# A retention layer and a two-layer feed-forward on one core: an order table per engine, one more block of layer 1 in seven products, queries loaded in token pairs, and paced loads at the head

## The chip, the core and the metric

One core of a Trainium2 chip runs the whole program. The metric is device time in microseconds (us), the median of repeated executions; lower is better. Before the change three runs took 283.76, 284.01 and 282.91 us, so the median is 283.76 us.

The engines are named as in the profile: PE multiplies matrices (PEld loads its weights), DVE and POOL work on vectors, ACT evaluates functions, SP issues most of the transfers. SBUF is the on-chip memory with 128 partitions, PSUM the eight banks (here `bk`) that PE writes.

## The reference

```python
def _attn_ref(q, k, v):                     # 8 batches, 8 heads, 576 tokens, 64 wide
    scores = scale * np.matmul(q, k.transpose(0, 1, 3, 2))
    gamma = 1.0 - 2.0 ** (-5.0 - np.arange(H))
    Dmat = np.where(rel >= 0, gamma[:, None, None] ** rel[None, :, :], 0.0)
    return np.matmul(scores * Dmat[None], v)

def _moe_ref(x, w_in, w_out):               # x: 4608 x 512, w_in: 512 x 2048, w_out: 2048 x 512
    h = x @ w_in
    g = h * np.cos(h)
    return g @ w_out
```

The result of the first function, with the heads put side by side, is the `x` of the second. There is no softmax: the decay factors into a weight of the query's position and one of the key's position, so earlier tokens can be summed up in a 64x64 state for each head.

## The kernel before

**Tiling.** The 4608 tokens are cut into nine blocks of 512. Each block is two units `(b, g)` of 256 tokens, g = 0 or 1, of two batches; the ninth block gathers the last 64 tokens of all eight batches. For each unit the kernel loads q, k and v into staging buffers (`stgq`, `stgk`, `stgv`, `load`), scales them to bf16 with the weights of their positions (`natk`, `natv`, `qnat`, in `unit`), turns k and q round (`kt`, `qt`: on PE with `tpe` in the first two blocks, by transposing transfers in `txb` after that), multiplies keys with queries (`scores`), masks the result on DVE with a triangle of ones (`pt <- bk, tr`, L714), sums keys times values into states (`states`, copied by ACT to `sba`, `sbb`, `sbr` in `snap`), and adds masked scores times values and queries times states (`outputs`). ACT and DVE copy that to `xt`, the block's input of layer 1.

A unit is "coarse" where a chunk is 128 tokens, held as 64 partitions times a pair of neighbouring tokens (`y` is the place in the pair), and "fine" where a chunk is 64 tokens. Coarse units are those of batches 0 and 1 and the units (2,0) and (3,0); ten units are fine. In a fine unit `y` is the half of 128 tokens, and q, k and v each come in two transfers of 256 KB, whose runs in DRAM are 64 numbers (256 bytes); a coarse unit's load is one transfer of 512 KB with runs of 128 numbers.

**Layer 1 and layer 2.** `mlp1(j, f, ...)` makes one of the 16 slices of 128 hidden columns of a block with four products of 512 columns (L879), then ACT's sine shifted by a quarter turn gives the cosine (L888) and DVE multiplies (L891) into `gt`. Blocks in `SEVEN` (4 to 8) do layer 1 by Strassen and Winograd's scheme instead: `xsums` makes three sums `xs` of the block's input and overwrites a part of `xt` (DVE), `wsums1` makes the sums `tx` of `w_in` once and overwrites a part of `win` (half of them on POOL, half on DVE), and `seven1(j, g, ...)` for each of four column groups does seven products of four matmuls of 256 columns (L1008), with ACT copying partial sums (`sq`, and `bk <- bk`, L939), DVE adding (`sq <- bk, sq`, L991) and DVE or POOL multiplying into `gt` (L997). Layer 2 does all nine blocks that way (`wsums`, `wino2`, L1148), and the results go out through `os`.

**What sets the order.** The program is a list of tasks. `Graph.run` walks through a model of the five engines with durations and due times written into the code, picks among the ready tasks of each engine the one with the best priority (`prios`, moved by the table `SHIFT`), and thereby fixes, on the host and before anything runs, the order of every engine's instructions; `FETCHES`, `AHEAD`, `BOND` and `DUE` tune its choices. The chip then executes each engine's list in order, with semaphore waits where data demand them. Where the model sees PE idle for over 0.4 us early on, `emit` puts products of a constant matrix there (`warm`, L500).

**The head.** Six loads (q, k, v of the units (0,0) and (1,0)) are at the front of SP's list and wait for nothing. The four slabs of `w_in` (`load_w`, issued from POOL, cast on the way) wait for certain loads (`SLABS`); the loads of the unit (0,1) wait for slab 2 (`NEXT`), the slabs of `w_out` for the keys of (1,1), the loads of (2,0) for the third slab of `w_out`. On SP, DMA loads are issued one after the other as soon as their staging buffer is free.

Of the kernel before, what the change touches and what calls it, by code (L numbers as in the profile page):

```python
# [6 lines left out]
ALU = mybir.AluOpType  # L7
# [123 lines left out]
class Graph:  # L131


    BACKLOG = 2500
    AHEAD, FETCH = 2000, 6500
    DUE = ("ses/0.1",)
# [49 lines left out]
    @staticmethod  # L186
    def fetch(at):
        return next(f for end, f in Graph.FETCHES if at < end)

    FETCHES = ((30000, 11500), (55000, 9500), (68000, 10200), (104000, 7800), (118000, 13000), (205000, 8800), (1e9, 6500))  # L190
    MARK = 213
    ENTER, LEAVE, BOND = 95, 105, 2000
# [5 lines left out]
    @staticmethod  # L198
    def fill(gap, seen):
        return int(0.6 * (gap - 150) / 220 if seen else (gap - 300) / 430)  # L200

    def first(self, t):
        need = {}
        for b in t.allocs:
            need[b.pool] = need.get(b.pool, 0) + 1
        return all(b in self.fifo[b.pool][:need[b.pool]] for b in t.allocs if b.pool in self.fifo)
# [19 lines left out]
    def shift(self, table):  # L226

        i = 0
        for n in range(0, len(table), 3):
            i += ord(table[n]) - 35  # L230
            x = (ord(table[n + 1]) - 35) * 90 + ord(table[n + 2]) - 35
            self.tasks[i].prio += 10 * (x - 4050)

    def reset(self):
        for t in self.tasks:
            t.start, t.wait = None, len(t.deps)
            t.parts[0][4].pop("push", None)
            for b in t.bufs:
                b.slot, b.left, b.free = None, len(b.tasks), 0.0
        self.pools = {p: [0.0] * len(f) for p, f in self.pools.items()}  # L240
        self.holder = {p: [None] * len(f) for p, f in self.pools.items()}
        self.fifo = {p: list(q) for p, q in self.queues.items()}

    def run(self):
        self.reset()
        free = {e: 0.0 for e in ("pe", "act", "dve", "pool", "sp")}
        ready = {e: [] for e in free}
        seen, asked, whole = 20, {}, [False] * 8
        dma_free, port_free = 0.0, {"dve": 0.0, "pool": 0.0}
        est, order, last, mode, held = {}, [], None, "", None  # L250
        for t in self.tasks:
            est[t] = 0.0
            if not t.wait:
                ready[t.eng].append(t)

        def slots(t):

            need, when = {}, 0.0
            for b in t.allocs:
                need[b.pool] = need.get(b.pool, 0) + 1  # L260
                if b.pool in self.fifo and b not in self.fifo[b.pool][:need[b.pool]]:
                    return None
# [7 lines left out]
        def pick(e):  # L270
            cand = []
            for t in ready[e]:
                if e == "pe" and held and t is not held and (t.then or t.name[:3] != "ses"):
                    continue
                a = slots(t)
                if a is None:
                    continue
                s = max(free[e], est[t], a)
                if e == "pe" and t.count:
                    k = (seen + t.count - 443) // 256  # L280
                    if k >= 0 and 443 + 256 * k > seen and k in asked:
                        s = max(s, asked[k] + self.fetch(asked[k]) - t.dur * (443 + 256 * k - seen) / t.count)
                if t.port:
                    s = max(s, port_free["pool" if e == "dve" else "dve"])
                if t.dma is not None and e != "pool":
                    s = max(s, dma_free - self.BACKLOG)
                cand.append((s, t))
            if e == "pe" and not held:
                due = [t for t in ready[e] if all(any(f is not None and f <= free[e] + 1500 for f in self.pools[b.pool])
                                                  for b in t.allocs if b.pool != "bk") and self.first(t) and sum(b.pool == "bk" for b in t.allocs) > 2 - (t.name in self.DUE) and est[t] <= free[e] + 1500]  # L290
                due = [t for t in due if t.prio <= min(x.prio for x in ready[e]) + self.AHEAD]
                if due:
                    d = min(due, key=lambda t: t.prio)
                    cand = [(s, t) for s, t in cand if t is d or not any(b.pool == "bk" for b in t.allocs)]
                    mine = [s for s, t in cand if t is d]
                    if mine:
                        cand = [(s, t) for s, t in cand if t is d or s + t.dur <= mine[0] + 150]
            if not cand:
                return None
            t0 = min(s for s, t in cand)  # L300
            slack = 60 if e == "pe" else 40
            return min(((s, t) for s, t in cand if s <= t0 + slack), key=lambda c: (c[1].prio - self.BOND * (e == "pe" and self.switch(mode, c[1].name) == 0 and mode[:3] == "ses"), c[0]))

        n = 0
        while n < len(self.tasks):
            best = None
            for e in free:
                c = pick(e)
                if c and (best is None or c[0] < best[0]):
                    best = c  # L310
            if best is None:
                rest = [(t.name, t.eng, [b.pool for b in t.allocs]) for e in ready for t in ready[e]]
                keep = {p: [b and [(t.name, t.eng) for t in b.tasks if t.start is None] for b in h] for p, h in self.holder.items()}
                raise RuntimeError(f"the scheduler is stuck: {self.pools} {free} {[x for x in rest if x[0][:3] == 'ses']} {rest[:12]} {keep}")
            s, t = best
            e = t.eng
            if e == "pe":
                s = max(s, free[e] + self.switch(mode, t.name))
            gap = s - free["pe"]
            ready[e].remove(t)  # L320
            t.start, t.order = s, n
            n += 1
# [7 lines left out]
            if e == "pe":  # L330
# [5 lines left out]
                if k >= 0 and k not in asked:  # L336
                    asked[k] = s + t.dur * max(0, 128 + 256 * k - seen) / max(1, t.count)
                seen += t.count
            mark = 0
            for b in t.allocs:  # L340
# [8 lines left out]
                self.holder[b.pool][i] = b  # L349
# [7 lines left out]
            for b in t.bufs:  # L357
                b.left -= 1
                b.free = max(b.free, done + (230 if e == "pe" else 170))
                if not b.left:  # L360
                    self.pools[b.pool][b.slot] = b.free
                    self.holder[b.pool][b.slot] = None
            order.append(t)
            for o in t.succ:
# [3 lines left out]
                if not o.wait:  # L368
                    ready[o.eng].append(o)
# [5 lines left out]
class Kernel:  # L375
# [8 lines left out]
    SEVEN = (4, 5, 6, 7, 8)  # L384
# [3 lines left out]
    SHIFT = (  # L388
        "$|KLw3?#U,,G3(j'Xw'Q/$X((Oe$6_6w'8cY/cu/am-@X&h2/fT&^Z)u,'bK'Z/$Zt$X5)W0%Wo$Si)LO&Q8)V?&GC&>H&Xd&J="
        "&_;%hW$BL&Jk&Q#(Y3$CR&Ec&R3&I_&jf&Gz)Fi,Ul)X(&H\\%L3&V6'U{(R|$T'&K6&[,%Ev-0w%mf%hO'oe$fT$CQ%pN(^l+EV"  # L390
        "$8I*--'%V$=d$:1%=@$=-$Xp&.:$21&Yx$tv%kW$nq+wV*Sm)B_/?^&Ej)9[&,4&>V&LX&Wy)X+$Jj%ED$JH$WK&YT$1A)*k,#k"
        "$_*&3I+S^)PL$-y&9s$c%&-w(JS$<|&]L'LL'M.;=A&D<&;3&#`);o,Y`&U`._`,Yp'-@%VS$`j%$$$Y+<B=$N7'dd'c%$KF&;b"
        "$fO'U`,I99^#'Ym)ND'E*$FW%Jk%F\\.2@,sT$aT)W>(^T%T_'[Q.80&N0,/B-^B$A{%\\J&:0%CC-Vp+Ao,0z%i-%#U$+D%X-'Vi"
        "%XA$Bd%SJ&^d$Z#$JA)Sk'?#$@B)@;/66$F]&3H%-)%5r&+/%.q'DM&Zp0TU2M.&A\\&q-*Tc(D5'4P%Pu$5^%UZ*%M(9P$9a';>"
        "*g{-\\Z'Wt&\\K?kt&VZ'MP%p9(%B8GP(I''8c%.#$\\f(Z*;Y15J6(>n$Aa*B|*\\Y:Yg$R;%Vb$7e&_R,&i0dx6\\S'AW*E\\%Xx%RH"
        "(XU(4Z&:S7Wo.So&Se,^[&Xc-`K$L\\%Wp$XH$T++Zd'U<*|K.Y7,Mb'Ar&#b%S_%To%\\p$J\\%=#'7E$fZ$)'(/G%.<(7U)Qx$k6"
        "&2]&.U':a$2Y%8O%$b'=S'BS-_0$XW)L8$Z=+-j$,w6|C$|K9xJ"
# [10 lines left out]
    def __init__(self, nc, es, q, k, v, w_in, w_out, out):  # L408
# [13 lines left out]
        self.TR = {2: sb("tr2", [128, 256], BF16), 1: sb("tr1", [128, 64], BF16)}  # L422
# [8 lines left out]
        self.whole = [False] * self.POOLS["bk"]  # L431
# [4 lines left out]
    def build(self):  # L436
        self.graph()
        self.G.prios()
        self.G.shift(self.SHIFT)
# [18 lines left out]
    def emit(self, order):  # L458
# [4 lines left out]
        whole = self.whole  # L463
        for t in order:
# [8 lines left out]
            for end, fn, r, w, kw in t.parts:  # L473
                kw = dict(kw)
                after = [i.ops[0] if isinstance(i, Task) else ops[i] for i in kw.pop("after", ())]
                if "push" in kw:
                    after.append(kw.pop("push").ops[0])
                sem = kw.pop("sem", None)
# [12 lines left out]
                ops.append(self.P.add(t.eng, fn, r=[phys(k) for k in r], w=[phys(k) for k in w], sem=sem, after=after))  # L491

# [13 lines left out]
    def constants(self):  # L506
# [29 lines left out]
        for ny in (2, 1):  # L536
            n = 64 * ny * ny
            for dst, up, name in ((self.TR[ny], 0, "tr"), (self.TB[ny], 1, "tb")):
                for y in range(ny):
                    dims = ([64, 2], [1, 64]) if ny == 2 else ([1, 64],)  # L540
                    P.add("pool", lambda e, dst=dst, up=up, ny=ny, y=y, n=n, dims=dims: e.affine_select(
# [780 lines left out]
```

## Time and profile before

| | before |
|---|---|
| median of three runs | 283.76 us (282.91 to 284.01) |
| span of the profiled execution | 282.1 us |
| PE busy | 274.2 us (97%), 4088 matmuls |
| DVE, ACT, POOL busy | 226.7 (80%), 174.9 (62%), 152.8 us (54%) |
| DMA packets | 133130, 49.90 MB |

The page gives the span of the profiled execution, from its first instruction to its last, and no device time of its own for it. The span is 1.66 us under the median of the timed runs, and that distance is carried along wherever a span is turned into a time. A matmul's busy time runs from its start to the end of its way through the array, so neighbouring ones overlap in the busy column; what one costs is the distance from start to start. Idle rows name the engine or transfer that ended the wait.

### The profile page before, as it was taken

Reading aid. Unit: us, or ns where it says so; the run is one execution under the profiler, and the core shown is the slowest. Engines: PE = TensorE matmul, PEld = TensorE weight load, DVE = VectorE, ACT = ScalarE, POOL = GpSimd, SP = SyncE. Lnnn points to the kernel's source line nnn. Section 1 sums busy time; section 2 is a strip of 40 time slices with the busy share of each in tenths; the row PEclk is TensorE's granted clock in tenths of the full one; section 3 lists DMA queues with packets and bytes.
Section 4 is the critical chain, followed back from the end, with each engine's and each line's share of the span. In section 5 each row is a group of like instructions: output and inputs, shape, how many; then the busy total and the mean of one; then the engine's idle time right before and its main releaser. Section 6 shows DMA issues by size and latency. Waiting matters only on the chain.

```text
span 282.1 us, 9696 instructions
## 1 busy us (share of the span) xinstructions
PE 274.2 (97%) x4088; PEld 216.5 (77%) x4088; DVE 226.7 (80%) x389; ACT 174.9 (62%) x355; POOL 152.8 (54%) x170
## 2 busy tenths in 40 slices
PE   7899999999999999999999999999999999999995
PEld 2567576888784476458888888888888889888884
DVE  4677979989937898898969786889689979579753
ACT  4357683672446744764578767785778577777620
POOL 5452870487334745258587949783779333433410
PEclk9999999999999999999999999999999999999999
DMA  7999999999999999999999999997857002200124
GB/s 194 265 224 279 244 179 228 283 199 193 192 260 224 207 188 258 188 200 188 293 159 260 184 244 207 231 208 169 169 145 151 3 2 77 77 0 2 74 77 149
DMA packets 133130, 49.90 MB, mean 177 GB/s; under 512 B 105440, under 2 KB 128992, under 8 KB 133088
## 3 DMA queue, kind: packets, MB, share of 16 engines
q1 hardware_dynamic: 128576, 44.84, 74.1%
q0 software_dynamic: 4224, 4.19, 9.3%
q8 instruction: 32, 0.52, 0.8%
q10 hardware_dynamic: 288, 0.26, 0.3%
q14 instruction: 10, 0.08, 0.1%
HBM read 36.70 MB, written 9.44 MB: 164 GB/s over the span
## 4 chain that ended last, share of the span: by engine, by line
PE 83%; DMA 8%; DVE 5%; POOL 1%; issue 1%; ACT 0%; SPq 0%; DVEq 0%
PE bk L1148 37%; PE bk L1008 22%; PE bk L879 14%; PE bk L675 8%; DMA stgv<-in_v_dram 3%; DMA wout<-in_moe_w_out_dram 3%; DVE pt L714 2%; DMA stgq<-in_q_dram 1%; PE bk L629 1%; PE bk L500 1%; DVE tw L1057 1%; POOL natv L605 1%; DVE gt L891 1%; DVE s L1079 1%; DVE s L1085 0%
## 5 line engine op out<-in xcount | busy, mean ns | idle before, releaser
L997 POOL TENSOR_TENSOR gt<-sq,cb 128x512 bf16<-128x512 f32 x40 | 46.1, 1161 | 38.5 <-ACT cb L993 24.6
L879 PE MATMUL bk<-xt,win 128*128 128x256 bf16 (+1 forms) x352 | 61.5, 321 | 0.2
L888 ACT ACTIVATE cb<-bk 128x256 bf16<-128x256 f32 (+1 forms) x88 | 41.7, 480 | 24.8 <-PE bk L879 22.6
L891 DVE TENSOR_TENSOR gt<-bk,cb 128x256 bf16<-128x256 f32 (+1 forms) x88 | 46.3, 542 | 12.5 <-ACT cb L888 8.5
L605 POOL TENSOR_TENSOR qnat<-stgq,wq 128x512 bf16<-128x512 f32 x32 | 33.5, 1051 | 39.8 <-DVE s L1079 19.9
L605 POOL TENSOR_TENSOR natv<-stgv,wv 128x512 bf16<-128x512 f32 x36 | 37.8, 1055 | 18.9 <-PE bk L675 4.3
L879 PEld LDWEIGHTS bk<-xt,win 128*128 128x128 bf16 x352 | 32.8, 98 | 19.3 <-ACT xt L555 0.8
L1148 PE MATMUL bk<-tw,s 128*128 128x256 bf16 x288 | 36.2, 273 | 0.4 <-ACT os L555 0.2
L1148 PE MATMUL bk<-wout,gt 128*128 128x256 bf16 x288 | 36.1, 273 | 0.3 <-DMA wout<-in_moe_w_out_dram 0.3
L1148 PE MATMUL bk<-wout,s 128*128 128x256 bf16 x288 | 35.9, 273 | 0.0
L997 DVE TENSOR_TENSOR gt<-bk,cb 128x512 bf16<-128x512 f32 x40 | 27.3, 687 | 9.5 <-ACT cb L993 6.9
L1008 PE MATMUL bk<-xt,win 128*128 128x256 bf16 x240 | 34.9, 273 | 0.0
L991 DVE TENSOR_TENSOR sq<-bk,sq 128x512 f32<-128x512 f32 x40 | 27.0, 686 | 9.3 <-ACT sq L555 4.3
L714 DVE TENSOR_TENSOR pt<-bk,tr 128x512 bf16<-128x512 f32 x48 | 30.7, 682 | 2.5 <-PE bk L675 2.4
L993 ACT ACTIVATE cb<-sq 128x512 bf16<-128x512 f32 x40 | 25.0, 630 | 11.3 <-DVE sq L991 11.0
L1148 PEld LDWEIGHTS bk<-tw,s 128*128 128x128 bf16 x288 | 28.0, 98 | 4.5 <-DVE tw L1057 0.3
L555 ACT ACTIVATE sn<-bk 128x512 f32<-128x512 f32 (+1 forms) x29 | 16.2, 565 | 24.0 <-PE bk L1148 22.2
L1148 PEld LDWEIGHTS bk<-wout,s 128*128 128x128 bf16 x288 | 27.6, 98 | 4.3 <-DVE gt L891 0.2
L1148 PEld LDWEIGHTS bk<-wout,gt 128*128 128x128 bf16 x288 | 27.7, 98 | 3.8 <-DMA wout<-in_moe_w_out_dram 0.5
L993 ACT ACTIVATE cb<-bk 128x512 bf16<-128x512 f32 x40 | 23.9, 600 | 8.6 <-PE bk L1008 7.2
L556 POOL CAST natk<-stgk 128x512 bf16<-128x512 f32 x34 | 20.9, 627 | 13.7 <-DMA stgk<-in_k_dram 8.4
L1137 DVE TENSOR_TENSOR os<-bk,sn 128x512 f32<-128x512 f32 (+1 forms) x28 | 18.5, 665 | 10.1 <-PE bk L1148 9.0
(80 smaller groups left out, 428.4 us busy)
## 6 DMA issues: line engine op xcount, KB each, us to landing
out_dram<-os SPq DMA_DIRECT2D x16, 512.0 KB, 4.6
stgq<-in_q_dram SPq DMA_DIRECT2D x20, 256.0 KB, 5.1
stgv<-in_v_dram SPq DMA_DIRECT2D x20, 256.0 KB, 5.0
stgk<-in_k_dram SPq DMA_DIRECT2D x20, 256.0 KB, 5.5
stgq<-in_q_dram SPq DMA_DIRECT2D x6, 512.0 KB, 6.9
stgk<-in_k_dram SPq DMA_DIRECT2D x6, 512.0 KB, 6.9
stgv<-in_v_dram SPq DMA_DIRECT2D x6, 512.0 KB, 7.2
win<-in_moe_w_in_dram POOLq DMA_DIRECT2D x4, 512.0 KB, 8.5
```

What stands on the lines that cost most here:

```text
L556: return self.one(eng, dur, lambda e: e.tensor_copy(dst(), src()), r=r, w=w, port=eng == "pool", **kw)
L605: self.one(eng, 610 if eng == "dve" else 1030, lambda e, out=out, inp=inp, tab=tab, col=col, hs=hs: e.tensor_tensor(out(), inp(), ap(tab, ...
L675: return lambda e: e.matmul(out(), lhs(), rhs(), start=start, stop=True, skip_group_check=True)
L714: self.one("dve", 610, lambda e, r=r, b=b, pt=pt: e.tensor_tensor(ap(self.at(pt), 1024, 0, 128, 512 * r, [64 * ny * ny, 8 // ny // ny], [1 ...
L879: inst = e.matmul(ap(self.at(bk), 512, 0, 128, 0, [1, n]), ap(self.WIN, 4 * DFF, 0, 128, c * DFF + 128 * f, [1, 128]), ap(self.at(xt), 204 ...
L888: self.one("act", n - 15, lambda e: e.activation(ap(self.at(cb), TB, 0, 128, 0, [1, n]), ap(self.at(bk), 512, 0, 128, 0, [1, n]), AF.Sin, ...
L891: self.one("dve", 75 + n / 0.96, lambda e: e.tensor_tensor(ap(self.at(gt), NF * TB, 0, 128, f * TB + 256 * h0, [1, n]), ap(self.at(bk), 51 ...
L991: self.one("dve", 610, lambda e: e.tensor_tensor(half(src), self.at(bank).ap(), half(src), ALU.add), r=[(bank,)], w=four(src))
L993: self.one("act", 530 if name else 490, lambda e: e.activation(self.at(cb).ap(), ap(self.at(src), size, 0, 128, 0, [1, 512]), AF.Sin, bias ...
L997: self.one(eng, 1120 if name else 610, lambda e: e.tensor_tensor(ap(self.at(gt), NF * TB, 0, 128, (8 * n + 2 * g) * TB + 256 * h, [TB, 2], ...
L1008: inst = e.matmul(ap(self.at(bank), 512, 0, 128, 256 * f, [1, 256]), l(c, f), rr(c), stop=True, skip_group_check=True, start=(first and f ...
L1148: inst = e.matmul(place(bank, tt), l(f, tt), rr(f), stop=True, skip_group_check=True, start=(first and f == 0 and tt < len(bank)))
```

## The change

Four things are changed together.

First, `run` no longer chooses. A new table `ORDER` gives each task a rank (`lay`), each engine's tasks are sorted by it, and `run` only works out when each would start. `first`, `fetch`, `pick`, `SHIFT`, `DUE`, `AHEAD` and `BOND` go. All five engines' lists are thereby new from the first few instructions on.

Second, block 3 joins `SEVEN`, so `wsums1` and the pair of units behind it move one block forward.

Third, the queries of the ten fine units are loaded as coarse ones are, one transfer of 512 KB with runs of 128 numbers. Their columns are then pairs of neighbouring tokens, so `queries` picks 32 columns of each parity for a chunk, a third triangle `tr3` masks the scores in that column order, and the copies to `xt` put the columns back in order (`128x8x2x32` instead of `128x2x4x64`).

Fourth, a load that SP issues and whose modelled start is before 45 us (`PACED`) waits until the load two places before it on SP has landed.

In the built program PE's list has 4137 matmuls instead of 4088 in the kernel's lines: 64 products of 512 columns of L879 go, 112 of 256 columns come, the scores' and outputs' counts are the same, and the constant products are 25 instead of 24. At the head SP's order starts q, k, v, q, k, v as before; on POOL the first slab of `w_in`, which stood ahead of the first keys and values, now stands behind the values of (0,0). PE does both first units, (0,0) and (1,0), before any product of layer 1; before, 24 products of layer 1 of 256 columns stood among those of (1,0).

```diff
-    BACKLOG = 2500
-    AHEAD, FETCH = 2000, 6500
-    DUE = ("ses/0.1",)
+    BACKLOG, FIRST = 4000, 6000
+    FETCH = (3200, 1500, 2550)
...
-    def shift(self, table):
...
+    def lay(self, table):
+
+        rank = iter(range(0, len(table), 2))
+        for t in self.tasks:
+            n = next(rank)
+            t.prio = (ord(table[n]) - 35) * 90 + ord(table[n + 1]) - 35
...
+        todo = {e: sorted((t for t in self.tasks if t.eng == e), key=lambda t: -t.prio) for e in free}
...
-    SEVEN = (4, 5, 6, 7, 8)
+    SEVEN = (3, 4, 5, 6, 7, 8)
...
+    PACED = 45000
+    ORDER = (
...
-        self.G.shift(self.SHIFT)
+        self.G.lay(self.ORDER)
...
+                if t.eng == "sp" and t.dma is not None and t.start < self.PACED:
+                    after += loads[-2:-1]
...
+                if t.eng == "sp" and t.dma is not None:
+                    loads.append(ops[-1])
...
-            elif fine:
+            elif fine and which != "q":
                 rows = [(0, 128, 512 * y, 1, u[0], 256 * u[1] + 128 * y) for y in range(2)]
...
-                rs = [(stg, i) for i in ((2 * y, 2 * y + 1) if fine else range(4))]
+                rs = [(stg, i) for i in ((2 * y, 2 * y + 1) if fine and which != "q" else range(4))]
...
+    def queries(self, u, qt, r, s, c, y):
+
+        o = c * 128
+        if u[1] == 2:
+            return ap(self.at(qt), 1024, 64 * r, 64, o + 64 * s + 512 * y, [1, 64])
+        if self.fine(u):
+            return ap(self.at(qt), 1024, 64 * r, 64, o + 64 * y + 32 * s, [512, 2], [1, 32])
+        return ap(self.at(qt), 1024, 64 * r, 64, o + 64 * s, [512, 2], [1, 64])
...
-                            rhs)))
+                            rhs, start=n == 0)))
...
-                ap(self.TR[ny], 64 * ny * ny, 0, 128, 0, [0, 8 // ny // ny], [1, 64 * ny * ny]), ALU.mult),
-                r=[(b,)] + [("tr", ny, y) for y in range(ny)], w=[(pt, r)])
+                ap(self.TR[tr], 64 * ny * ny, 0, 128, 0, [0, 8 // ny // ny], [1, 64 * ny * ny]), ALU.mult),
+                r=[(b,)] + [("tr", tr, y) for y in range(ny)], w=[(pt, r)])
...
-                if rem:
-                    o, d = (64 * s, 1) if fine else (s, 2)
-                    dst = lambda o=o, d=d: ap(self.at(xt), 2048, 0, 128, 1024 * half + o, [128, 2], [256, 4], [d, 64])
+                if fine:
+                    dst = lambda s=s: ap(self.at(xt), 2048, 0, 128, 1024 * half + 64 * s, [128, 8], [1, 2], [2, 32])
+                    src = lambda s=s: ap(self.at(ob[s]), 512, 0, 128, 0, [64, 8], [32, 2], [1, 32])
+                elif rem:
+                    dst = lambda s=s: ap(self.at(xt), 2048, 0, 128, 1024 * half + s, [128, 2], [256, 4], [2, 64])
```

206 lines of the change are left out of this document (90 added, 116 removed).

## The prediction

> **What bounds the kernel now.** I read the page's totals and its chain first, then what PE waited for, then the engines' busy time by stretch. First the totals, and the chain's shares by engine:
>
> ```profile
> span 282.1 us, 9696 instructions
> PE 274.2 (97%) x4088; PEld 216.5 (77%) x4088; DVE 226.7 (80%) x389; ACT 174.9 (62%) x355; POOL 152.8 (54%) x170
> PE 83%; DMA 8%; DVE 5%; POOL 1%; issue 1%; ACT 0%; SPq 0%; DVEq 0%
> ```
>
> PE is busy in 97% of the span and carries 83% of the chain. The rest of the chain is DMA and DVE, and the next views place it.
>
> ```profile
> PE bk L500 <- DVE lg L526: 1.1, 1, 1.1
> PE bk L675 <- DVE pt L714: 1.0, 2, 0.9
> PE bk L629 <- DVE qnat L605: 0.7, 1, 0.7
> PE bk L675 <- POOL natv L605: 0.6, 1, 0.6
> PE bk L675 <- DVE kt L556: 0.4, 2, 0.2
> PE bk L1148 <- DMA wout<-in_moe_w_out_dram: 0.3, 1, 0.3
> PE bk L1148 <- ACT os L555: 0.2, 1, 0.2
> PE bk L1148 <- DVE tw L1057: 0.2, 1, 0.2
> ```
>
> These are all waits of PE: in us, times, longest. They sum to 4.5 us.
>
> ```profile
> core 0: us, PE busy (x) PEld busy (x) DVE busy (x) ACT busy (x) POOL busy (x), PEclk, DMA share, GB/s
> 0.00:21.70 21.70, 18.54 (x287) 10.87 (x287) 13.40 (x37) 10.15 (x21) 10.83 (x26) 1.00 1.07 227
> 21.70:47.00 25.30, 23.88 (x322) 16.25 (x319) 20.48 (x42) 17.24 (x39) 13.39 (x16) 1.00 1.11 225
> 47.00:84.00 37.00, 36.70 (x562) 30.86 (x560) 31.88 (x60) 18.19 (x42) 19.60 (x23) 1.00 1.12 233
> 84.00:238.00 154.00, 153.90 (x2550) 121.81 (x2549) 131.08 (x205) 104.75 (x207) 95.73 (x94) 1.00 0.90 182
> ```
>
> PE's idle time is 3.16 us in the first stretch, 1.42 in the second, 0.30 in the third, 0.10 in the fourth. So from 47 us on the kernel costs what PE's instructions cost, and only before that is there time that an order can win or lose. There the transfers are the limit: their share is over 1 from the start.
>
> **Block 3 in seven products.** The price of a matmul is the distance between starts.
>
> ```profile
> 111.92 3.62 PE L879 MATMUL bk<-xt,win 128*128 128x512 bf16 x16
> 115.47 0.45 PE L675 MATMUL bk<-qt,kt 64*64 64x64 bf16 x32
> ...
> 103.95 1.04 PE L1148 MATMUL bk<-tw,s 128*128 128x256 bf16 x8
> 104.92 0.45 PE L675 MATMUL bk<-pt,natv 64*64 64x64 bf16 x32
> ...
> 273.78 3.66 PE L1148 MATMUL bk<-wout,s 128*128 128x256 bf16 x32
> 277.27 1.91 PE L1148 MATMUL bk<-tw,gt 128*128 128x256 bf16 x16
> ```
>
> 32 products of 256 columns take 277.27 - 273.78 = 3.49 us, 0.109 each. Eight of them would take 0.87, but from 103.95 to 104.92 lie 0.97: going over to the small products of the attention costs 0.10. Less that, 16 products of 512 columns take 115.47 - 111.92 - 0.10 = 3.45 us, 0.216 each. The change takes out 64 x 0.216 = 13.8 us and puts in 112 x 0.109 = 12.2: **-1.6 us**, in a stretch where PE never waits.
>
> What comes with it on other engines, for the stretch of block 3:
>
> ```profile
> L997 POOL TENSOR_TENSOR gt<-sq,cb 128x512 bf16<-128x512 f32 x40 | 46.1, 1161 | 38.5 <-ACT cb L993 24.6
> L991 DVE TENSOR_TENSOR sq<-bk,sq 128x512 f32<-128x512 f32 x40 | 27.0, 686 | 9.3 <-ACT sq L555 4.3
> L555 ACT ACTIVATE sq<-bk 128x512 f32<-128x512 f32 x40 | 23.4, 598 | 1.6 <-PE bk L1008 1.5
> ...
> 98.00:126.00 28.00, 28.00 (x453) 17.75 (x452) 25.32 (x39) 15.98 (x33) 13.90 (x15) 1.00 1.16 209
> ```
>
> POOL gets 8 x 1.16 = 9.3 us and is busy for 13.9 of 28: hidden. ACT gets eight copies and four seeds, about 12 x 0.60 = 7.2 us, on 16.0 of 28: hidden. DVE trades 16 multiplications for eight additions and eight multiplications at about the same 0.69, and gets four sums of about half a us: +2 on 25.3 of 28, which leaves 0.7 of slack. That is the tight place. The sums of `w_in` (`wsums1`) move one block forward, past the loads' casts on POOL and the masks on DVE. I take 0, with up to +1.5 us if DVE falls behind there.
>
> **Switches and constant products.** PE's new order goes into or out of attention products 78 times instead of 82: 4 x 0.10 = **-0.4 us**. It has two more constant products inside the head's dense part (three against one, 0.216 each): **+0.4**.
>
> **The head.** These are its loads and the steps of the second unit.
>
> ```profile
> stgq<-in_q_dram SPq DMA_DIRECT2D x1, 512.0 KB, 4.2
> stgk<-in_k_dram SPq DMA_DIRECT2D x1, 512.0 KB, 5.4
> ```
>
> ```profile
> 0.79 0.47 SPq L566 DMA_DIRECT2D stgq<-in_q_dram  x1
> 1.33 0.56 SPq L566 DMA_DIRECT2D stgk<-in_k_dram  x1
> ...
> 5.26 0.96 POOL L859 DMA_DIRECT2D win<-in_moe_w_in_dram  x1 [2.17 <-DMA stgq<-in_q_dram]
> ...
> 8.71 2.04 POOL L605 TENSOR_TENSOR natv<-stgv,wv 128x512 bf16<-128x512 f32 x2 [1.28 <-ACT kt L555]
> ...
> 17.10 2.04 POOL L605 TENSOR_TENSOR natv<-stgv,wv 128x512 bf16<-128x512 f32 x2 [0.40 <-DMA stgv<-in_v_dram]
> ...
> 17.75 1.47 PE L500 MATMUL bk<-one 128*128 128x512 bf16 x6
> ...
> 19.73 1.03 PE L879 MATMUL bk<-xt,win 128*128 128x256 bf16 x8
> ...
> 21.74 6.89 PE L879 MATMUL bk<-xt,win 128*128 128x256 bf16 x48
> ```
>
> The first load lands at 0.79 + 4.2 = 5.0 us, the second at 1.33 + 5.4 = 6.7. A load alone takes 4.2, and in a full queue one follows the other after 1.7. Paced in twos, the queue gives two per 4.2 us, 2.1 each. So the landings become 5.0, 6.7, 9.2, 10.9, 13.4 and 15.1 for the values of (1,0), where before they landed just ahead of 17.10. Before, the first slab of `w_in` was issued at 5.26 and shared the engines with them; now POOL issues it behind the values of (0,0), at about 9.2 + 2.04 = 11.2. A slab's work is bounded by this row:
>
> ```profile
> q0 software_dynamic: 4224, 4.19, 9.3%
> ```
>
> 9.3% of 282.1 us over eight slabs is 3.3 us each, all engines together. If all of it goes ahead of the last load, that lands at 18.4; if none, at 15.1. I take 16.0, near the lower end, since the last two loads are issued at 9.2 and 10.9, ahead of the slab.
>
> From that landing to the start of the long row of layer 1 at 21.74 the trace has 4.7 us, of which the eight products at 19.73 fill 0.9. Without them 3.8: the long row starts at 19.8, between 18.9 and 22.2. But it starts with less behind it: 24 products of layer 1 stood before it, 24 x 0.109 = 2.6 us, so level would be 21.7 - 2.6 = 19.1. That is **+0.7 us**, with ends of -0.2 and +3.1.
>
> In return those 24 products stand in a row as long as the loads of (0,1) and (1,1) are under way, and PE has work where it idled: 1.42 + 0.30 us after 21.7. I take half, **-0.9**, with ends of 0 and -1.7. What a longer wait there would look like is a rival.
>
> [...]
>
> **Queries in pairs.** The page has `stgq` in two halves:
>
> ```profile
> stgq<-in_q_dram SPq DMA_DIRECT2D x20, 256.0 KB, 5.1
> stgq<-in_q_dram SPq DMA_DIRECT2D x6, 512.0 KB, 6.9
> ```
>
> Twenty transfers become ten, so SP has ten fewer to issue and 20480 runs of 256 bytes become 10240 of 512. A first half is there up to 1.8 us later. PE waits for no query load after the head, so both count nothing: POOL's spare time covers the delay, 40% of it idle after 47 us. The copies to `xt` change their pattern, not their size; the third triangle adds two small selections on POOL near 3 us, where POOL waits for the first load at 5.26 anyway.
>
> **Sum.** -1.6 - 0.4 + 0.4 + 0.7 - 0.9 = -1.8 us. Span 280.3; with the 1.66 us between span and median (283.76 - 282.1) that is **282.0 us**. Its own range by its ends: -1.6 - 0.2 - 1.7 = -3.5 to -1.6 + 3.1 + 1.5 = +3.0.
>
> **Rivals.** *The head closes up.* A new order over all five lists takes most of the idle time before 47 us, not half of that after 21.7: 3.16 + 1.42 us less the 1.1 before PE's first product, and the values of (1,0) land at 15.1. -1.6 - 0.2 - 3.5 = -5.3: 278.5. For it: DMA is full to 47 us, so which transfer is first decides everything. Against it: six loads and four slabs have to land whatever the order.
>
> *The slabs come too late.* The first slab moves from 5.26 to 11.2, the loads of (0,1) hang on slab 2 and the keys of (1,1) on theirs and, paced, on another landing; the slabs of `w_out` hang on those. If the head's transfers end 4 us later, the first product of layer 2, which even before waited for `wout` (0.3 us above), waits for it: slower from 1.8 us of delay on, +2 at 4 us: 286.
>
> *DVE becomes the bound at block 3.* 25.3 + 2 of 28 us, and the sums of `w_in` earlier in a stretch where DVE has 31.88 of 37 us. PE idles 1 to 3 us between 70 and 126; with +2.5 the net is +0.7: 284.5.
>
> *Nothing in the end.* What the products save, the queue and DVE take back: 283.5.
>
> [...]
>
> **Chances.** The forecast 0.40, the closed head 0.24, late slabs 0.16, DVE 0.09, nothing 0.08, clock 0.03. What a measurement can tell here is about 0.5%, 1.4 us: faster means under 282.3, slower over 285.2. Of the forecast's own range somewhat over half lies under 282.3 (0.23) and nearly all the rest within the bounds (0.14); with the closed head faster is 0.47. Slower is the late slabs, a third of DVE and the forecast's tail, 0.22. Same is the rest, 0.31. The range from 279.0 to 285.8 leaves out the tails of the closed head and of late slabs, one in ten on each side.
>
> **What would show it.** Right: no idle PE in the stretch of block 3; the long row of layer 1 starting at 19 to 21 us; less idle PE from 21.7 to 47. Wrong: a wait of PE for `wout` or `win` of over a us, waits for DVE between 70 and 126 us, or values of (1,0) landing after 17.1. The step I trust least is the landing at 16.0.

## The result, and the profile after

| | before | after |
|---|---|---|
| median | 283.88 us (4 runs, 282.91 to 284.31) | 297.72 us (4 runs, 295.47 to 298.78) |
| ratio | | 1.0465, 95% interval 1.0405 to 1.0525 |
| span of the profiled execution | 282.1 us | 296.5 us |
| PE busy, and span less that | 274.2, 7.9 us | 277.3, 19.2 us |

The kernel became 4.65% slower: 13.8 us, where 1.8 us less was forecast. Here and below a ratio leaves out the executions over 1.5% above the fastest of the same kernel, a median does not. The page of the changed kernel, its totals and the row of the DMA queue for instructions (packets, MB, share of 16 engines):

```profile
span 296.5 us, 9755 instructions
PE 277.3 (94%) x4137; PEld 224.1 (76%) x4137; DVE 231.3 (78%) x394; ACT 178.2 (60%) x367; POOL 161.6 (54%) x180
q8 instruction: 32, 0.52, 0.8%
```

PE idles 11.3 us more than before and is also busy 3.1 us longer. The busy time by stretch, cut at the same places as before, and then in three stretches in which the granted clock is about one half:

```profile
0.00:21.70 21.70, 14.02 (x187) 7.64 (x187) 11.32 (x32) 7.63 (x13) 7.70 (x24) 0.84 0.81 190
21.70:47.00 25.30, 20.54 (x254) 13.27 (x258) 13.32 (x28) 12.46 (x30) 12.21 (x15) 0.87 0.84 186
47.00:84.00 37.00, 34.15 (x463) 28.06 (x456) 28.98 (x60) 18.53 (x47) 16.00 (x19) 0.91 0.93 199
84.00:238.00 154.00, 152.91 (x2584) 125.73 (x2574) 131.52 (x203) 106.06 (x215) 104.70 (x105) 1.00 0.91 194
...
12.00:19.10 7.10, 5.83 (x107) 4.10 (x107) 5.06 (x9) 2.13 (x5) 1.67 (x3) 0.52 0.96 193
22.30:29.20 6.90, 3.98 (x77) 2.62 (x78) 0.21 (x1) 0.59 (x2) 4.29 (x6) 0.51 0.60 155
49.70:56.50 6.80, 6.11 (x43) 3.90 (x43) 2.36 (x5) 2.98 (x6) 1.29 (x2) 0.50 1.08 176
```

The loss lies ahead of 84 us. Idle PE there is 7.68, 4.76 and 2.85 us, before 3.16, 1.42 and 0.30. The DMA share, over 1 before, is 0.81, 0.84 and 0.93: the transfers were the limit, and now they pause. From 84 to 238 us PE idles 1.1 us, before 0.1. PE's longest waits in the whole span, in us, times, longest:

```profile
PE bk L658 <- POOL natv L588: 7.5, 2, 6.0
PE bk L658 <- issue: 3.3, 2, 2.8
```

Where the 6.0 comes from is seen in the timelines of SP and POOL and in the queues from 15.5 to 20.5 us. First SP's issue of the values of (1,0) before, then SP's and POOL's rows after:

```profile
6.68 1.74 SPq L566 DMA_DIRECT2D stgv<-in_v_dram  x1
...
6.79 0.37 SPq L549 DMA_DIRECT2D stgq<-in_q_dram  x1
9.31 0.37 SPq L549 DMA_DIRECT2D stgk<-in_k_dram  x1
11.93 0.37 SPq L549 DMA_DIRECT2D stgv<-in_v_dram  x1
...
11.42 0.96 POOL L852 DMA_DIRECT2D win<-in_moe_w_in_dram  x1
14.24 0.60 POOL L539 CAST natk<-stgk 128x512 bf16<-128x512 f32 x1 [1.87 <-DMA stgk<-in_k_dram]
14.80 0.75 POOL L852 DMA_DIRECT2D win<-in_moe_w_in_dram  x1
23.13 2.04 POOL L588 TENSOR_TENSOR natv<-stgv,wv 128x512 bf16<-128x512 f32 x2 [7.59 <-DMA stgv<-in_v_dram]
```

```profile
q0 software_dynamic: 742, 0.74, 90.3%
q1 hardware_dynamic: 597, 0.30, 27.2%
```

The values of (1,0) are issued at 11.93 and land at 23.06, after 11.1 us; a load alone takes 4.2 (the kernel before's first, issued at 0.79). Two slabs of `w_in` are issued around it, at 11.42 and at 14.80, and when it lands 1040 of their 1056 packets have been moved. Before, the same load was issued at 6.68, behind five others in a full queue, and landed at 17.03. So 5.25 of the 6.0 us by which it comes later are the later issue; pacing gave up a place in the queue, and the slabs beside the load kept it from making that up. From 15.5 to 20.5 us their queue (q0) and the loads' queue (q1) got on at a like pace, 742 packets to 597, but a slab's packet took 0.903 x 80 / 742 = 0.097 us of an engine and a load's 0.272 x 80 / 597 = 0.036. So here the load got 0.8 of a small packet through for each long one. That is no fixed ratio: in the kernel before, from 10 to 14 us, the two queues' packets are 437 to 1141, and in e3, below, from 37.3 to 46 us, 1472 to 472. Then what PE makes of it, in its timeline:

```profile
25.23 0.64 PE L658 MATMUL bk<-natv,natk 64*64 64x64 bf16 x16 [6.02 <-POOL natv L588]
28.88 7.71 PE L872 MATMUL bk<-xt,win 128*128 128x256 bf16 x60
50.39 0.32 PE L658 MATMUL bk<-natv,natk 64*64 64x64 bf16 x5 [2.85 <-issue]
```

The long row of layer 1 starts at 28.88 instead of 21.74. The idle time before 50.39 is put down to no data ("issue"). Counted in the trace, PE has stopped there after its 933rd instruction (matmuls and weight loads), and the queue for instructions moved one packet of 16 KB from 47.94 to 48.90. There are 32 such packets (0.52 MB) for 8274 instructions of PE, one for about 259. The row of the queue doesn't name an engine; that it is PE's own program that comes over the DMA engines, which the loads fill, is the account that these numbers suggest.

### The profile page after: what moved, and what is told of

It reads as the page before. It is cut to its first block, busy times and chain, and to the rows that moved or that the text cites. A ratio compares the mean times of both kernels' runs of the same rounds, so it can differ in the third digit from the quotient of the medians.

```text
span 296.5 us, 9755 instructions
## 1 busy us (share of the span) xinstructions
PE 277.3 (94%) x4137; PEld 224.1 (76%) x4137; DVE 231.3 (78%) x394; ACT 178.2 (60%) x367; POOL 161.6 (54%) x180
## 4 chain that ended last, share of the span: by engine, by line
PE 82%; DMA 7%; DVE 3%; POOL 3%; issue 2%; ACT 1%; SPq 0%; POOLq 0%; DVEq 0%
PE bk L1141 36%; PE bk L1001 22%; PE bk L872 15%; PE bk L658 8%; DMA stgv<-in_v_dram 4%; DMA stgk<-in_k_dram 2%; DMA stgq<-in_q_dram 2%; POOL natv L588 1%; POOL qnat L588 1%; DVE s L1072 1%; DVE gt L884 1%; POOL gt L990 1%; DVE pt L707 1%; PE bk L612 1%; PE bk L481 1%
## 5 line engine op out<-in xcount | busy, mean ns | idle before, releaser
L990 POOL TENSOR_TENSOR gt<-sq,cb 128x512 bf16<-128x512 f32 x48 | 55.1, 1162 | 30.6 <-ACT cb L986 19.3
L872 PE MATMUL bk<-xt,win 128*128 128x256 bf16 (+1 forms) x288 | 48.5, 320 | 1.1 <-ACT cb L881 1.0
L884 DVE TENSOR_TENSOR gt<-bk,cb 128x256 bf16<-128x256 f32 (+1 forms) x72 | 34.3, 508 | 15.3 <-ACT cb L881 11.8
L881 ACT ACTIVATE cb<-bk 128x256 bf16<-128x256 f32 (+1 forms) x72 | 31.3, 459 | 24.4 <-PE bk L872 23.1
L1001 PE MATMUL bk<-xt,win 128*128 128x256 bf16 x288 | 40.8, 273 | 0.3 <-ACT sq L538 0.3
L872 PEld LDWEIGHTS bk<-xt,win 128*128 128x128 bf16 x288 | 27.8, 101 | 14.2 <-ACT cb L881 1.5
L990 DVE TENSOR_TENSOR gt<-bk,cb 128x512 bf16<-128x512 f32 x48 | 32.4, 684 | 7.6 <-ACT cb L986 4.9
L984 DVE TENSOR_TENSOR sq<-bk,sq 128x512 f32<-128x512 f32 x48 | 32.4, 684 | 6.7 <-PE bk L1001 6.3
L538 ACT ACTIVATE sq<-bk 128x512 f32<-128x512 f32 x48 | 28.6, 600 | 9.4 <-PE bk L1001 7.2
L986 ACT ACTIVATE cb<-sq 128x512 bf16<-128x512 f32 x48 | 29.8, 633 | 4.5 <-DVE sq L984 3.1
L1001 PEld LDWEIGHTS bk<-xt,win 128*128 128x128 bf16 x288 | 27.7, 98 | 4.1 <-ACT sq L538 0.6
```

The costliest lines, as they stand in the source:

```text
L538: return self.one(eng, dur, lambda e: e.activation(dst(), src(), AF.Copy), r=r, w=w, **kw)
L872: inst = e.matmul(ap(self.at(bk), 512, 0, 128, 0, [1, n]), ap(self.WIN, 4 * DFF, 0, 128, c * DFF + 128 * f, [1, 128]), ap(self.at(xt), 204 ...
L881: self.one("act", n - 15, lambda e: e.activation(ap(self.at(cb), TB, 0, 128, 0, [1, n]), ap(self.at(bk), 512, 0, 128, 0, [1, n]), AF.Sin, ...
L884: self.one("dve", 75 + n / 0.96, lambda e: e.tensor_tensor(ap(self.at(gt), NF * TB, 0, 128, f * TB + 256 * h0, [1, n]), ap(self.at(bk), 51 ...
L984: self.one("dve", 610, lambda e: e.tensor_tensor(half(src), self.at(bank).ap(), half(src), ALU.add), r=[(bank,)], w=four(src))
L986: self.one("act", 530 if name else 490, lambda e: e.activation(self.at(cb).ap(), ap(self.at(src), size, 0, 128, 0, [1, 512]), AF.Sin, bias ...
```

## The experiments

**e1: the changed kernel without pacing.**

```diff
-    PACED = 45000
+    PACED = 0
```

> The changed kernel with the pacing of loads taken out and all else kept. Theory (pacing is the cause: it has the values of (1,0) issued at 11.9 us, behind the first slab of w_in, so that they share the DMA engines with two slabs and land at 23.1): those values land before 16 us, the clock stays at 1.0, and the time falls by 10 us or more, to 280 to 286. Rival (the new order as such, slabs first on POOL and both first units ahead of layer 1, is at fault): the values still land after 20 us or PE idles elsewhere, and the time stays over 292.

Measured: 286.92 us (10 runs, 285.3 to 291.39) against 284.17; ratio 1.0077, 1.0043 to 1.0110, which is 2.2 us. The six loads land at 4.99, 6.80, 8.61, 10.41, 12.22 and 13.92. So pacing costs some 11 of the 13.8 us (1.0465 against 1.0077), as the theory says, though the median ends just above its 286. The profiled execution took 289.94 us, more than eight of the other nine, so its stops need not be typical. It shows 5.5 us of waits without a releaser; the two ahead of 84 us are:

```profile
19.52 0.74 PE L658 MATMUL bk<-pt,natv 64*64 64x128 bf16 x18 [1.67 <-issue]
41.73 0.25 PE L658 MATMUL bk<-natv,natk 64*64 64x64 bf16 x5 [2.63 <-issue]
```

and, among the queues' rows from 17.0 to 18.5 us, an instruction packet:

```profile
q8 instruction: 1, 0.02, 4.1%
```

By count they follow PE's instructions 441 and 933; the second is the number at which the paced kernel stopped. In e2, next, PE's list is the same and neither stop is there.

**e2: pacing only from the seventh load on.**

```diff
+                if t.eng == "sp" and t.dma is not None and t.start < self.PACED and len(loads) > 5:
```

> The changed kernel with only its first six loads unpaced; the later ones still wait for the load two places before. Theory (the first six are what costs): as with no pacing at all, within 3 us, 281 to 288. Rival (pacing of the loads of (0,1) and (1,1) costs as much, and it is what delays the slabs of w_out and PE's stop of 3 us at 47): 290 or more, with that stop still there.

Measured: 289.64 us (one run), between the two branches. The values of (1,0) land at 13.97. PE waits 3.3 us for the queries of (1,1), which are issued at 33.46 just ahead of two slabs of `w_out` (33.73 and 35.55), and land at 40.87, 7.4 us later. That is the same sharing, with `w_out` in the place of `w_in`. The time is 2.7 us over e1's median, but within the spread of e1's runs, so the wait is shown and its price is not.

**e3: the kernel before with pacing and nothing else.** The same lines were put into the old `emit`.

> The kernel before with nothing but the pacing added. Theory (the pacing costs by itself, whatever the order): slower by 5 us or more, since the loads of (1,0) are issued later and share with a slab that is issued at 5.3 as before: 288 to 296, with a fall of the clock if PE idles long enough. Rival (it costs only together with the slab's new place on POOL): within 2 us of the kernel before.

Measured: 294.02 us (one run) against 284.17, so 9.9 us, as the theory expected. SP's issue of the values of (1,1), their cast on POOL, and PE behind it:

```profile
34.46 0.37 SPq L571 DMA_DIRECT2D stgv<-in_v_dram  x1
...
46.07 1.04 POOL L610 TENSOR_TENSOR natv<-stgv,wv 128x512 bf16<-128x512 f32 x1 [7.76 <-DMA stgv<-in_v_dram]
...
48.65 0.61 PE L634 MATMUL bk<-idn,qnat 128*128 128x128 bf16 x4 [6.62 <-POOL qnat L610]
```

The load is issued at 34.46 and lands at 46.0, after 11.5 us, with four slabs of `w_out` issued from 34.74 to 38.3. Before, it was issued at 28.68, ahead of every slab of `w_out` (the first at 32.53), and landed at 35.18. So pacing costs about as much in another place and without the table: the issue that waits for a landing comes 5.8 us later, with the slabs beside it. The cast of the queries for which PE waits is behind that of the values in POOL's list.

**e4: more constant products in the waits of the head.** 45 products are added where PE waits for keys and values.

> The changed kernel with 45 more constant products put into PE's four long waits before 26 us, which computes the same. Theory (the late values are the first cause and the half clock the second, worth about 3 us in the head): the clock stays at 1.0 up to 47 us and the time falls by 2 to 4 us, to 293 to 296. Rival (the clock is most of the loss): it falls by 7 or more. Second rival (the clock costs nothing because PE waits anyway): within 1 us of the changed kernel.

Measured: 297.17 us (one run), inside the changed kernel's spread of 295.47 to 298.78. The mean granted clock rises from 0.965 to 0.994, and no gain is seen. PE's last long wait of the head:

```profile
51.00 0.40 PE L617 MATMUL bk<-idn,qnat 128*128 128x128 bf16 x4 [4.06 <-POOL qnat L593]
```

The values of (1,0) still land at 22.60, so the half clock is not what makes them late. The long row of layer 1 starts at 26.94 instead of 28.88. That is lost again: the queries of (1,1) take 10.05 us, from 39.78 to 49.83, where in the changed kernel the same load took 4.1, from 41.61 to 45.74. Here the work done faster waited for the next landing, and as this landing also came later, the run does not tell what the clock is worth by itself.

**e5: block 3 in seven products, alone, in the kernel before.** The list scheduler stays; its table of shifts is moved along so that each step keeps its own.

```diff
-    SEVEN = (4, 5, 6, 7, 8)
+    SEVEN = (3, 4, 5, 6, 7, 8)
```

> The kernel before, its list scheduler and its head unchanged, with block 3 added to SEVEN (the table of shifts moved along, so that each step keeps its own). The theory of the prediction: 64 products of 0.216 us go and 112 of 0.109 come in a stretch in which PE never waits, so 1.6 us less, about 282.4 against 284.0. The rival, DVE as the bound at block 3: PE gets idle time of 1 to 3 us between 70 and 126 us and the time is 284 to 286. A third outcome, no difference within 0.5 us, would mean that the sum of block 3 is given back elsewhere in the list.

Measured: 289.18 us against 283.75; ratio 1.0193, 1.0167 to 1.0220: slower by more than any branch allowed. PE's busy time falls to 273.1 us, and its idle time rises to 14.0. The busy time from 126 to 154 us, then PE's waits between 84 and 238 us:

```profile
126.00:154.00 28.00, 24.63 (x440) 20.33 (x437) 23.52 (x36) 20.48 (x43) 21.65 (x23) 1.00 1.06 205
```

```profile
PE bk L1031 <- DVE sq L1014: 1.4, 1, 1.4
PE bk L1171 <- DVE os L1160: 0.9, 1, 0.9
PE bk L1031 <- DVE pt L737: 0.8, 1, 0.8
PE bk L1031 <- ACT xt L578: 0.7, 1, 0.7
```

PE idles 3.4 us where it had idled for nothing, for sums, masks and copies of DVE and ACT. This is the mechanism of the rival, DVE as the bound, in the old list, but mostly behind the place that it named: from 70 to 126 us PE idles 0.9 us. In the changed kernel the whole stretch from 84 to 238 us has 1.1 us of idle PE, so there the new order carries block 3. (The list scheduler also reorders other steps once its tasks change; how much of the 5.4 us is that isn't separated.)

**e6: queries in token pairs, alone, in the kernel before.**

> The kernel before with only the queries of the ten fine units loaded as token pairs (and the third triangle and the copies that belong to it); the list up to 40 us is unchanged. The prediction counted this at nothing: 284.0 within 0.7 us. The rival is that a first half that is there up to 1.8 us later stalls PE somewhere between 50 and 230 us: 285 to 287, with a wait of PE for qnat or qt. Less DMA time could also give a gain of up to 1 us.

Measured: 289.64 us against 283.75; ratio 1.0205, 1.0183 to 1.0228, more than either branch allowed. PE's idle time is 14.3 us, in many small waits, of which the longest after 47 us are

```profile
PE bk L700 <- DVE pt L749: 1.4, 1, 1.4
PE bk L1043 <- ACT bk L974: 0.7, 1, 0.7
```

None of them is a wait for a query. Some 2 us more lie ahead of 47 us (6.6 us of idle PE against 4.6), where the values of (1,0) land at 18.26 instead of 17.03 though they are issued at the same time; that isn't explained. Ten tasks fewer send the list scheduler another way. That this is what costs is likely, not shown; the price of the loads themselves can't be read from this run.

**e7: paced, but the slabs behind the casts.** Only POOL's order is changed: the first two slabs of `w_in` come after the casts of (1,0).

```diff
+        for i, rank in ((39, 3), (46, 4), (45, 5), (60, 6), (61, 7)):
+            self.tasks[i].prio = rank
```

> The changed kernel, paced, with one thing moved on POOL: the casts of (1,0)'s keys and values stand ahead of the first two slabs of w_in instead of behind them. The theory that the two slabs beside it made the values of (1,0) land at 23.06 says: they land at 15 to 16.5, the 6.2 us wait of PE at 19 us goes down to under 1, and the first slab, issued at about 18, lands at 21 to 23, so the long row of layer 1 starts at 22 to 24 instead of 28.9; the time is 291 to 295, since pacing still holds the queries of (1,1) to over 43 us. The rival, that the load is late by itself (paced, or in a queue that is full anyway), says that the values land after 20 us and the time stays at 297 to 299.

Measured: 291.39 us (one run), inside 291 to 295. SP's issue of the values of (1,0), POOL's cast and its slabs, and PE's long row:

```profile
11.37 0.37 SPq L551 DMA_DIRECT2D stgv<-in_v_dram  x1
...
15.92 2.04 POOL L590 TENSOR_TENSOR natv<-stgv,wv 128x512 bf16<-128x512 f32 x2 [1.38 <-DMA stgv<-in_v_dram]
17.90 3.19 POOL L854 DMA_DIRECT2D win<-in_moe_w_in_dram  x4
...
26.97 7.59 PE L874 MATMUL bk<-xt,win 128*128 128x256 bf16 x52 [0.68 <-DMA win<-in_moe_w_in_dram]
```

The same paced load, without slabs beside it, takes 15.85 - 11.37 = 4.5 us. That shows the slabs beside it as the cause of its 11.1 us. The wait of 6 us is gone, and the row of 52 starts at 26.97, behind 16 products at 23.95. What is left to 286.9 was not taken apart; the slabs now come late (the DMA share up to 21.7 us is 0.63, and the second slab, for which PE waits there, lands at 26.93), and PE waits 2.1 us at 43 for values.

**e8 and e9: without pacing, with 40 more PE instructions at the start.** 20 products of 16 columns go ahead of the first constant products, where PE waits anyway.

```diff
+        more = 0 if hasattr(self, "shifted") else 20
...
+            for _ in range(more):
+                e.matmul(ap(self.at(self.wb), 512, 0, 128, 0, [1, 16]), self.ONE.ap(), ap(self.ONE, 128, 0, 128, 0, [1, 16]), ...)
```

> The changed kernel without pacing, with 20 products of 16 columns (40 PE instructions, about 1 us of work where PE waits for its first load anyway) put in at the very start. In the unpaced kernel PE stops after instruction 441 (1.9 us) and after 933 (2.8 us). [...] If they are waits for data, they stay at the same place in the work and move to about 481 and 973. The time: 286 to 288 either way.

> The kernel of e8 again (the changed kernel without pacing, with 20 small products at the start), timed. If its 283.42 us holds, the stops for instructions cost the unpaced kernel 3 to 4 us, and the rest of the change is worth about nothing net: 283 to 284 against 284.0, ratio 0.995 to 1.001. If the one run of e8 was a lucky one, it is 285 to 287 like the unpaced kernel.

Measured: 283.42 us once, then 283.57 us (12 runs) against 283.62; ratio 0.9987, 0.9956 to 1.0018, no difference. The expectation of e8 was wrong: the stops neither moved to instructions 481 and 973, as waits for data would have, nor stayed after 441 and 933: in its profile they are gone. The packet is there from 13.15 to 14.35 us, where in e1 it came from 17.26 to 18.23. With 40 more instructions ahead of the work the packet came 4.1 us sooner; what asks for it, no view shows. In e9's profile one stop is left:

```profile
37.09 0.30 PE L664 MATMUL bk<-pt,natv 64*64 64x128 bf16 x7 [0.30 <-issue]
```

It is short, 1.3 us after the end of a packet at 35.83, and by count again after instruction 933, which is 40 instructions earlier in the work than in e1. So the stop keeps its number and not its place, which speaks for a stop for instructions and against a wait for data. Small products of a microsecond in all, put into idle time, are worth some 2.6 us (1.0077 against 0.9987). e8's totals, its stretches, and one of its waits of PE:

```profile
span 281.7 us, 9792 instructions
PE 271.1 (96%) x4157; PEld 220.5 (78%) x4157; DVE 230.9 (82%) x394; ACT 177.8 (63%) x367; POOL 161.4 (57%) x180
```

```profile
0.00:21.70 21.70, 17.60 (x312) 10.95 (x313) 13.62 (x37) 10.84 (x21) 11.22 (x28) 1.00 1.05 215
21.70:47.00 25.30, 23.69 (x295) 16.32 (x293) 20.30 (x43) 16.54 (x40) 13.62 (x16) 1.00 1.12 226
47.00:84.00 37.00, 35.92 (x583) 30.34 (x582) 31.92 (x58) 16.99 (x42) 20.00 (x23) 1.00 1.17 243
```

```profile
PE bk L664 <- DMA qt<-qnat: 1.1, 1, 1.1
```

The granted clock is 1.00 in all three, and PE's work is 3.1 us shorter than before although 20 products are in it (1.8 in e9's profile, 2.5 in e10's); its idle time is 10.6 us, 2.7 longer. What the products save, the new order loses in waits. One of them, 1.1 us at 76 us (0.3 in e9, 0.7 in e10), is for turned queries (`qt`), a wait that the kernel before did not have.

**e10: the same 20 products behind instruction 443.** They stand just ahead of the first product of layer 1.

> The changed kernel without pacing, with the 20 small products not at the start but just ahead of the first product of layer 1, that is after PE's instruction 443. If the stops come from the instruction stream, the first (after instruction 441, 1.9 us) stays as it was in the unpaced kernel, since nothing ahead of it is changed, and only the second (after 933, 2.8 us) goes down or away, since its piece is asked for 20 products earlier: 284.5 to 286.5. If the 20 products helped in e8 by what they do to the clock or to PE's wait for the first load, nothing is gained here: 287 to 288 with both stops.

Measured: 283.47 us (one run), a microsecond under what was expected. As expected the first stop stays after instruction 441, and it is the only one left:

```profile
PE bk L669 <- issue: 1.1, 1, 1.1
```

The second is gone. Nothing ahead of 443 differs from e1, so the products help without a change to the clock ahead of 443 and without covering PE's first wait; their place in the instruction stream is the account that is left. It is one run, under all ten of e1. Its first stop is 0.6 us shorter than in e1's profile, and no half clock follows it; the same instructions gave no stop at all in e2, so the stops vary from one execution to the next.

**e11: pacing for the first six loads only.**

> The changed kernel with pacing for the first six loads only; the loads behind them are issued as soon as they may. Pacing of the later loads alone cost 289.6 - 286.9 = 2.7 us. If the two parts add up, this is 297.7 - 2.7 = 295; if the late values of (1,0) cover what the later pacing costs, it is 297 to 298, and if the later pacing is the larger part once the head is late, under 293. The values of (1,0) land at 23 and PE waits 6 us at 19 in any case.

Measured: 300.33 us (one run), 2.6 more than the changed kernel and outside all three branches. The values of (1,0) land at 23.51 and PE waits 6.7 us. So taking the pacing of the later loads away gained nothing here, and the parts of pacing don't add up. One run doesn't settle why, or whether it is a loss; in its profile a half clock lasts for 17.1 us on end.

**e12: paced, with the 20 products at the start.**

> The changed kernel as it is, paced, with the 20 small products at the start. Under pacing PE stops after instruction 933 (3.0 us at 47.4), but there the queries of (1,1) also land only at 45.7 and are cast behind that. The theory that the data are late by pacing anyway says that the stop for instructions goes and a wait for qnat takes its place: 295.5 to 298. If the instruction stream is the larger part also here, it is 292 to 294.

Measured: 296.10 us (one run), inside 295.5 to 298. No stop for instructions is left, and the data take its place:

```profile
PE bk L664 <- POOL natv L594: 4.9, 2, 3.4
PE bk L618 <- POOL qnat L594: 4.7, 1, 4.7
```

That fits the theory, but two landings changed as well, so the price of the stops under pacing can't be read from it. The values of (1,0), issued at 12.03 with the same two slabs beside them, landed at 19.79, after 7.8 us instead of 11.1; the queries of (1,1) took 10.3 us, from 38.87 to 49.15, instead of 4.1. And the time lies within the changed kernel's own spread.

The order table by itself was not measured. Nor was an edit that the diff shows and the list of four changes does not name: the scores' products set their start flag only on the first product of a bank (`start=n == 0`).

## Why the prediction was wrong

**What bounds the kernel** was read rightly: only the head can win or lose, and there the transfers are the limit. The loss is there, in the DMA share that falls below 1.

**The paced landings** were worked out as 5.0, 6.7, 9.2, 10.9 and 13.4 for the first five loads, and came at 5.12, 6.77, 9.29, 11.91 and 14.18. The price of a load alone, 4.2 us, holds for the third; the fourth and fifth took 5.1 and 4.9. e1 and e3 put some 11 and 9.9 us on pacing.

**The values of (1,0) are the step that failed.** The prediction took 16.0, "near the lower end, since the last two loads are issued at 9.2 and 10.9, ahead of the slab", with 18.4 as the upper end if one slab of 3.3 us goes ahead. It was the step trusted least, and the sign named for it, a landing after 17.1, is the one that came. The load was issued at 11.93, behind the first slab's issue at 11.42 and not ahead of it, because the fourth load took 5.1 us; and POOL's list has a second slab, behind the keys' cast at 14.24, still ahead of the values' cast. The prediction's own rows give the right answer with two slabs: 11.93 + 4.2 + 2 x 3.3 = 22.7, measured 23.06. That it comes so near is partly luck, since in e12 the load landed at 19.79 with the same two slabs beside it. From there to the long row it took 5.8 us instead of 3.8, at a granted clock of 0.51 (22.3 to 29.2). So the row started at 28.88, and against the prediction's level of 19.1 the +0.7 us became +9.8. e7 shows it from the other side: no slab beside the load, 15.85. The kernel before already held the price: there the first slab stood beside the fifth and sixth load, and they landed at 14.61 and 17.03, behind a fourth at 10.34, so 4.3 and 2.4 us apart where e1 has 1.8.

**"Idle PE after 21.7 half gone", -0.9 us, had the wrong sign.** Idle PE grew by 3.3 us from 21.7 to 47 and by 2.6 us from there to 84. Without pacing the sign is open: over both stretches +1.0 us in e8, +0.5 in e9, and -0.8 in e10. Two causes weren't in the prediction at all: loads paced into the slabs of `w_out` (e2, e3), and stops for PE's instructions, to which the 2.6 us between e1 and e9 point.

**Block 3, switches and constant products** were forecast at -1.6 us of PE's work. Without pacing there is 1.8 to 3.1 us less of it (e8 to e10), so the saving is real and at least as large as forecast; the parts weren't measured singly. That DVE would keep up held in the changed kernel, but only with the new order: e5 shows what it is worth without.

**Queries in pairs** at nothing: nearly so. e8 to e10 have one wait of 0.3 to 1.1 us for them at 76 us.

**The rivals.** The late slabs ended on the right side for a neighbouring reason: `w_out` did land late, the first slab at 48.5 instead of 40.1, but PE's waits have no row for it; a load beside slabs was the bound, not a slab. The fall of the clock, at 0.03 among the chances, did come: the granted clock was 0.52, 0.51 and 0.50 in three stretches of some 7 us (12.0 to 19.1, 22.3 to 29.2 and 49.7 to 56.5). The mean clock of 0.965 over 296.5 us is 10.4 us of lost clock; what part of it counts stays open, since part fell on time in which PE waited anyway and e4's one run has a later landing in it. The closed head, at nearly a quarter the strongest rival, has nothing for it.

**The range** ended at 285.8 because a landing's worst case was bounded by one slab; with two slabs and the same sum it would have reached 282.0 + 22.7 - 16.0 = 288.7. The rest can be estimated from the profile, in the prediction's own terms: the long row +9.8; idle PE from the long row to 84 us 4.1 instead of 1.7, so +2.4; the third stretch of half clock (0.50), 6.1 us of busy PE, about +3.0; idle PE from 84 to 238 us +1.0; PE's work -1.6 as forecast. That is 14.6, beside 14.4 between the two profiled spans. The first term is 9.1 us worse than forecast, and that step is the bulk of the miss.

## What to carry to other kernels

Before a transfer is made to wait for another's landing, list what is issued between the two on every queue, and price the transfer with all of that beside it: loads that waited in a full queue ahead of the slabs landed 1.8 us apart, one issued among them took 11 where it takes 4.2 alone. The place in the queue was worth most of the delay here: the transfer that waited gave it up, and 5.25 of its 6.0 us are the later issue. An engine's instructions can be one of the transfers: here a packet of the queue for instructions ended 1.3 to 1.5 us ahead of PE's start after a stop (after, e1, e9). A stop without a releaser that kept its instruction number between two versions (933 in after, e1 and e9) was the sign that led to it, and some cheap instructions put ahead gained more than their own time (some 2.6 us for less than one). A change to the tasks of a list scheduler whose table was fitted step by step is a new schedule: single edits in e5 and e6 cost 5 to 6 us, where both edits under a table made for them cost nothing on balance (e9).

No version here beats both kernels: the change without pacing and with the stops removed (e9) is level with the kernel before.

## What was unexpected on the chip

A load of 512 KB beside casting slabs took 11.1 us (after) and 11.5 us (e3), alone 4.2: from 15.5 to 20.5 us in the changed kernel the two queues moved 742 and 597 packets, though one queue's packets lasted 0.097 us and the other's 0.036. The price was not a fixed one. The queries of (1,1), with a slab of `w_out` issued 0.27 us behind them each time, took 4.1 us (after), 5.2 (e7), 7.4 (e2), 10.1 (e4) and 10.3 (e12). The load ahead of them in their queue landed 1.7, 1.8, 2.1, 2.3 and 2.6 us after their issue, in the same order. So it seems that what is left of a load when the slab's packets begin goes at the slow pace; five runs suggest that, and none was made to test it.

The queue for instructions moved 32 packets of 16 KB while PE did 8274 instructions (after). The packet ahead of a stop itself took 0.96 us (after, from 47.94) and 0.97 (e1, from 17.26), PE went on 1.3 to 1.5 us after its end, and the stops were 0.3 to 2.9 us long. Where they came in the head it was after instruction 441 or 933, but not in every version or execution.
